# Attention with feature maps: token sums of the key features past 32 standing columns of ones, turned together with the key sums, and projection weights first on the load queue

## The chip, the cores and the metric

One core of a Trainium2 chip runs the whole program. The metric is device time in microseconds (us) from launch to end, as the median of several executions. Engines are named as in the profile: PE (TensorE, matmuls; PEld its weight loads), DVE (VectorE), ACT (ScalarE), POOL (GpSimd) and SP (SyncE, which here only issues DMAs). Each engine takes its instructions in the order in which the program gives them.

## The reference, cut to what matters

```
def phi(x):                                  # x: 8 batches, 8 heads, 576 tokens, 64
    proj = x @ w_phi                         # 64 -> 128 features
    proj = proj - max(abs(proj), last axis)
    return concat([exp(proj), exp(-proj)])   # 256 features
q_p, k_p = phi(q), phi(k)
kv  = einsum('bhsf,bhsd->bhfd', k_p, v)      # key sums, 256 x 64 for each batch and head
z   = sum(k_p, over tokens)                  # token sums, 256 for each batch and head
num = q_p @ kv ; den = q_p @ z + 1e-6
x   = num / den                              # 4608 tokens x 512
x   = (h - tanh(h)) @ w_out, h = x @ w_in    # first expert stage
out = ((x @ w1) * (x @ w2)) @ w3 @ w_out2    # second expert stage
```

Everything is 32-bit floating point. The change concerns `kv`, `z` and the loads at the start; the two expert stages are untouched.

## The kernel before, in words

The attention stage is `attention()`. A *step* is one head of a pair of batches: 1152 tokens in nine tiles of 128. There are 32 steps of keys; the queries of a step run one step behind its keys, so there are 33 passes and 297 tiles. The loop at L412 goes over *slots*, four tiles each, 75 with tiles and a few more to drain. Nine slots make four steps. The order of the work on each engine is the order in which this loop calls the parts; there is no planner.

In slot s, PE gets: `p_pe(s)` (projections of the queries on array rows 0 to 63 and of the keys on rows 64 to 127, L212), `t_pe(s-1)` (transposes of the query projections, L253), `kv_pe(s-2)` (key sums into a PSUM bank `kv`, two column tiles of 64, L290), `o_pe` of a step (numerators, L343, and denominators, L352, one half of the tokens a slot; eight slots of nine have one), and, if a step's key sums were finished in the slot before, `kv_turn` of that step. `kv_turn` transposes the two halves of the key sums with the identity (L325) and multiplies the four key-feature sums `ks`, 128 tokens x 128 features, as weights with one moving column of ones (L329), which gives four columns of token sums.

DVE gets in a slot: `kv_copy` (L320, the finished key sums from PSUM to `kvs`), maximum and difference of the queries (L219, L221), a store copy `st` (L364, every other half; the other halves go to ACT at L366), `kv_out` (L334, the turned sums from PSUM to `kvx`, of the step whose turn was in the slot before), part of the conversion of expert weights, maximum and difference of the keys, the rest of the conversion. `o_pe` of the next step reads `kvx`; in o_pe the denominators read each column of token sums broadcast to 32 weights (L349). ACT takes the exponentials (L232 keys, L274 queries), half of the store copies and parts of the conversion. POOL adds up `ks` over the tiles (L310, L314) and takes parts of the conversion.

`kv` has two PSUM banks, so `kv_pe` of a step needs `kv_out` of the step two before it. `qk` has two buffers; `load_step` (L194) issues the load of the step after next at the end of the slot with a step's last tile, on SP, behind the stores of the slot (two of numerators and four of denominators for each half). `wphi`, the projection weights, is loaded in two halves by ACT's queue (L400), the first `qk` whole by SP.

The last lines of a slot, before:

```
                todo_o = [(st, c, o_pe(st, c)) for st, c in o_at.get(s, [])]
                if turned is not None:
                    kv_turn(turned)
                some(99)
```

Of the kernel before, what the change touches and what calls it, by code (L numbers as in the profile page):

```python
# [8 lines left out]
F32 = mybir.dt.float32  # L9
# [7 lines left out]
B, H, S, D = 8, 8, 576, 64  # L17
F = 128
# [5 lines left out]
PT = 2 * S  # L24
TPP = PT // 128
NPAIR = NBP * H
# [27 lines left out]
def kernel(ctx, tc, qk_in, v_in, w_phi, w_in, w_out, w12, w3t_in, wo2, out):  # L54
    nc = tc.nc
    PE, ACT, DVE, POOL, SP = nc.tensor, nc.scalar, nc.vector, nc.gpsimd, nc.sync
# [14 lines left out]
    ident = const.tile([128, 128], F32, name="ident")  # L71
# [101 lines left out]
    def attention():  # L173
        with ExitStack() as es:
            pool = es.enter_context(tc.tile_pool(name="att", bufs=2))
            one = es.enter_context(tc.tile_pool(name="att1", bufs=1))
# [2 lines left out]
            ps_o = es.enter_context(tc.tile_pool(name="ps_o", bufs=2, space=PSUM))  # L179

            wphi = one.tile([128, F], F32, name="wphi")
            ones = one.tile([128, 1], F32, name="ones")
            n_steps = NPAIR + 1
            n_tiles = n_steps * TPP
            n_slots = (n_tiles + G - 1) // G
# [6 lines left out]
            qk, vv = {}, {}  # L192

            def load_step(st):  # L194
                qk[st] = pool.tile([128, PT], F32, tag="qk", name="qk")
                SP.dma_start(qk[st], qk_in[st])
                if st < NPAIR:
                    vv[st] = pool.tile([128, TPP + 1, D], F32, tag="v", name="v", bufs=3)
                    SP.dma_start(vv[st], v_in[st])
# [3 lines left out]
            def p_pe(g):  # L203
                for what, js in ((pq, q_js(g)), (pk, k_js(g))):
                    if js:
                        what[g] = ps_h.tile([128, 512], F32, tag="h", name="p").rearrange("p (t f) -> p t f", f=F)
                for j, n in enumerate(tiles_of(g)):
                    st, t = where(n)
                    c = slice(t * 128, (t + 1) * 128)
                    for what, js, r in ((pq, q_js(g), 0), (pk, k_js(g), 64)):  # L210
                        if j in js:
                            PE.matmul(what[g][:, j, :], qk[st][r:r + 64, c], wphi[r:r + 64], start=True, stop=True)  # L212
# [13 lines left out]
            def k_exp(g, sgn):  # L226
                js = k_js(g)
                if not js:
                    return
                if sgn == 0:  # L230
                    kp[g] = pool.tile([128, 2, G, F], F32, tag="kp", name="kp", bufs=3)
                ACT.activation(kp[g][:, sgn, span(js)], dk[g][:, span(js)], ACTF.Exp, scale=1.0 - 2 * sgn)  # L232

            def q_parts(g):

                runs = []
                for st, t, j in sorted((where(G * g + j)[0], ORDER[where(G * g + j)[1]], j) for j in q_js(g)):
                    if runs and runs[-1][0] == st and runs[-1][1] + len(runs[-1][2]) == t:
                        runs[-1][2].append(j)
                    else:  # L240
                        runs.append((st, t, [j]))
                return runs

            def t_pe(g):
                runs = q_parts(g)
                if not runs:
                    return
                d = dq.pop(g)
                pt[g] = ps_t.tile([128, 512], F32, tag="tr", name="tr")
                at = 0  # L250
                for st, t, js in runs:
                    for j in js:
                        PE.transpose(pt[g][:, at * 128:(at + 1) * 128], d[:, j, :], ident)  # L253
                        at += 1
# [21 lines left out]
            kv_ps, ks, kvx = {}, {}, {}  # L276
# [39 lines left out]
            kvs = {}  # L316

            def kv_copy(st):
                t = kvs[st] = pool.tile([128, 2 * F], F32, tag="kvs", name="kvs")
                DVE.tensor_copy(t, kv_ps[st][:, :2 * F])  # L320

            def kv_turn(st):
                ps = kv_ps[st]
                for s in range(2):
                    PE.transpose(ps[:, 252 + s * 128:380 + s * 128], kvs[st][:, s * F:(s + 1) * F], ident)  # L325
                for b in range(2):
                    for s in range(2):
                        c = 508 + 2 * b + s
                        PE.matmul(ps[:, c:c + 1], ks[st][:, b, s, :], ones, start=True, stop=True)  # L329
                del kvs[st], ks[st]  # L330

            def kv_out(st):
                t = kvx[st] = pool.tile([128, 260], F32, tag="kvx", name="kvx")
                DVE.tensor_copy(t, kv_ps.pop(st)[:, 252:512])  # L334

            def o_pe(st, c):

                ps = ps_o.tile([128, 512], F32, tag="o", name="o")
                x, w = qp[st], kvx[st - 1]
                for s in range(2):  # L340
                    for b in range(2):
                        c0 = b * S + c * CW
                        PE.matmul(  # L343
                            ps[b * D:(b + 1) * D, :CW], w[:, s * 128 + b * D:s * 128 + (b + 1) * D],
                            x[:, s, c0:c0 + CW], start=s == 0, stop=s == 1,
                        )
                for s in range(2):
                    for b in range(2):
                        z = w[:, 256 + 2 * b + s:257 + 2 * b + s].to_broadcast([128, 32])  # L349
                        for e in range(2):  # L350
                            r, c0 = 64 * b + 32 * e, b * S + c * CW + e * CE
                            PE.matmul(  # L352
                                ps[r:r + 32, CW:CW + CE], z, x[:, s, c0:c0 + CE], start=s == 0, stop=s == 1,
                                tile_position=(0, r),
                            )
                if c:
                    del qp[st], kvx[st - 1]
                return ps
# [37 lines left out]
                for d, fs in zip((0, 2, 3, 3, 4, 4), c):  # L396
                    extra[at + d] += fs

            for i in range(2):
                ACT.dma_start(wphi[i * D:(i + 1) * D], w_phi)  # L400
            load_step(0)
            load_step(1)
            DVE.memset(ones, 1.0)
            o_at = {}
# [3 lines left out]
                    o_at.setdefault(g + 2 + c, []).append((st, c))  # L408
            n_end = n_slots + 8
            ok = lambda g: 0 <= g < n_slots  # L410
            kv_done, turned, todo_o = None, None, []
            for s in range(n_end):  # L412
                x = list(extra[s])

                def some(n):
                    for _ in range(n):
                        if x:
                            x.pop(0)()

                if ok(s):  # L420
                    p_pe(s)
                if kv_done is not None:
                    kv_copy(kv_done)
                if ok(s - 1):
                    k_exp(s - 1, 0)
                    k_exp(s - 1, 1)
                    t_pe(s - 1)
                if ok(s):
                    dq[s] = p_max(s, pq, q_js(s), "q")
                for st, c, ps in todo_o:  # L430
                    bp = o_out(st, c, ps)
                    if bp == NBP - 1:
                        pending.extend([lambda: recip_load(NBP - 1), lambda: recip(NBP - 1)])
                    elif bp is not None:
                        recip_load(bp)
                        extra[s + 4].append(lambda bp=bp: recip(bp))
                if turned is not None:
                    kv_out(turned)
                some(2)
                turned = kv_done  # L440
                if ok(s - 1):
                    q_exp(s - 1, 0)
                    q_exp(s - 1, 1)
                    kv_sum(s - 1)
                kv_done = kv_pe(s - 2) if ok(s - 2) else None
                if ok(s):
                    dk[s] = p_max(s, pk, k_js(s), "k")
                todo_o = [(st, c, o_pe(st, c)) for st, c in o_at.get(s, [])]
                if turned is not None:
                    kv_turn(turned)  # L450
                some(99)
                for n in tiles_of(s) if ok(s) else ():
                    st, t = where(n)
                    if t == TPP - 1 and st + 2 < n_steps:
                        load_step(st + 2)
                i = s - n_slots // 2
                if 0 <= i < 8 * NK:
                    if i % 8 == 0:
                        xa = load_x(0, i // 8)
                    elif i % 8 == 4:  # L460
                        mul_x(*xa)
                    elif i % 8 == 6:
                        split_x(0, i // 8, xa[0])
# [509 lines left out]
    with tc.manual_schedule():  # L973
# [36 lines left out]
        def mul_x(a, r):  # L1010
            POOL.tensor_tensor(a, a, r, ALU.mult)
# [63 lines left out]
```

## Time and profile before

| | us |
|---|---|
| median of three runs | 1761.9 (1760.24 to 1765.2) |
| the profiled execution | 1764.12 |
| its span, first to last instruction | 1762.3 |
| PE busy in the span | 1716.5 (97%) |
| DVE busy | 1331.7 (76%) |
| POOL busy | 1007.1 (57%) |
| ACT busy | 927.2 (53%) |

The profile is of one execution. Attention ends at about 388 us of the span; the expert stages fill the rest. A busy share over the whole span mixes stages, so the rows below are taken from the attention stage, by stretch, by wait and by single instruction. "x16" behind an instruction is the number of rows merged; a 32-bit matmul has two rows, a transpose one.

### The profile page before, as it was taken

How to read it: one execution, taken by the hardware profiler on the slowest of the kernel's cores; microseconds unless marked ns; L12 is line 12 of the kernel's file. 1: busy time of each engine (PE TensorE's matmuls, PEld its weight loads, DVE VectorE, ACT ScalarE, POOL GpSimd, SP SyncE). 2: the span in 40 equal slices, each digit the busy share in tenths (PEclk: the TensorE clock that was granted, in tenths of full speed). 3: DMA queues.
4: the chain of work that ended last, by engine and by line, in shares of the span. 5: the costliest groups of instructions: out<-in, count | busy, mean ns of one | idle time of the engine just before them, and what ended most of it. 6: DMA issues, size and time to landing. Idle time of an engine off the chain costs nothing.

```text
span 1762.3 us, 30387 instructions
## 1 busy us (share of the span) xinstructions
PE 1716.5 (97%) x10608; PEld 1455.0 (83%) x10608; DVE 1331.7 (76%) x1910; ACT 927.2 (53%) x1881; POOL 1007.1 (57%) x966
## 2 busy tenths in 40 slices
PE   7999899999999999999999999999999999999999
PEld 5666666667878788878888878888999999999998
DVE  6777777849888798879899989664766666666664
ACT  4665566646676667666767776544332323222221
POOL 5777677736566677765666667225534353535341
PEclk9999999999999999999999999999999999999999
DMA  4444455522232324233434342635989898989886
GB/s 157 148 149 147 136 171 159 160 61 77 61 114 93 117 78 137 92 129 103 140 105 135 106 137 89 232 117 200 348 261 317 263 315 269 309 269 309 273 268 195
DMA packets 173161, 306.16 MB, mean 174 GB/s; under 512 B 21712, under 2 KB 57936, under 8 KB 173008
## 3 DMA queue, kind: packets, MB, share of 16 engines
q1 hardware_dynamic: 168960, 297.07, 52.1%
q10 hardware_dynamic: 4048, 7.15, 1.1%
q8 instruction: 84, 1.38, 0.3%
q14 instruction: 69, 0.57, 0.1%
HBM read 240.93 MB, written 63.21 MB: 173 GB/s over the span
## 4 chain that ended last, share of the span: by engine, by line
PE 81%; DVE 9%; DMA 4%; issue 2%; POOL 2%; ACT 1%; SPq 1%; DVEq 0%; ACTq 0%; POOLq 0%
PE h L477 18%; PE y L553 18%; PE q L808 14%; PE q L817 7%; PE pa L808 6%; PE p L212 3%; PE o L343 3%; PE o L817 3%; PE h L715 2%; PE kv L290 2%; PE o L352 2%; DVE u L507 1%; DMA qk<-in_qk 1%; DVE t L508 1%; PE tr L253 1%
## 5 line engine op out<-in xcount | busy, mean ns | idle before, releaser
L524 POOL TENSOR_TENSOR gl<-t,gh 128x512 fp32r<-128x512 f32 x144 | 201.5, 1399 | 178.4 <-ACT gh L523 118.5
L553 PE MATMUL y<-gh,w 128*128 128x512 f32 x936 | 237.2, 391 | 3.8 <-ACT gh L523 2.5
L808 PE MATMUL q<-w,w 128*128 128x384 f32 x1152 | 215.1, 334 | 0.0
L553 PEld LDWEIGHTS y<-gh,w 128*128 128x128 f32 x936 | 175.7, 188 | 42.1 <-ACT gh L523 3.5
L507 DVE SCALAR_TENSOR_TENSOR u<-s,u 128x512 f32<-128x512 f32 x144 | 201.0, 1396 | 4.7
L808 PEld LDWEIGHTS q<-w,w 128*128 128x128 f32 x1152 | 201.1, 188 | 0.0
L879 POOL TENSOR_TENSOR xa<-c,c 128x384 f32<-128x384 f32 x48 | 52.1, 1085 | 249.8 <-DVE c L878 179.3
L477 PE MATMUL h<-xa,w 128*128 128x512 f32 x780 | 189.0, 392 | 0.0
L497 ACT ACTIVATE u<-h 128x512 f32<-128x512 f32 x144 | 85.7, 595 | 185.0 <-PE h L477 178.5
L477 PEld LDWEIGHTS h<-xa,w 128*128 128x128 f32 x780 | 147.8, 190 | 31.4 <-issue 0.2
L508 DVE COPY_PREDICATED t<-m,u 128x512 f32<-128x512 uint32 x144 | 166.3, 1155 | 5.0
L219 DVE TENSOR_REDUCE m<-p 128x4 f32<-128x512 f32 (+1 forms) x145 | 98.8, 681 | 79.5 <-PE p L212 79.4
L477 PE MATMUL h<-xb,w 128*128 128x512 f32 x624 | 149.9, 389 | 0.0
L858 ACT ACTIVATE c<-pa 128x384 f32<-128x384 f32 x48 | 23.6, 492 | 237.3 <-PE pa L808 188.0
L232 ACT ACTIVATE kp<-dk 128x512 f32<-128x512 f32 x144 | 83.0, 626 | 109.4 <-DVE dk L221 78.2
L553 PE MATMUL y<-gl,w 128*128 128x512 f32 x468 | 132.0, 394 | 6.5 <-POOL gl L524 6.5
L477 PEld LDWEIGHTS h<-xb,w 128*128 128x128 f32 x624 | 117.1, 188 | 24.5
L135 POOL TENSOR_TENSOR et<-et,eraw 128x256 uint32<-128x256 uint32 x92 | 68.8, 748 | 112.3 <-ACT u L497 35.5
L504 DVE TENSOR_TENSOR t<-h,t 128x512 f32<-128x512 f32 x144 | 98.3, 683 | 42.4 <-ACT t L498 42.2
L505 DVE SCALAR_TENSOR_TENSOR u<-h,u 128x512 f32<-128x512 f32 x144 | 98.6, 684 | 32.8 <-ACT m L500 32.5
L817 PE MATMUL q<-w,w 128*128 128x384 f32 x612 | 112.8, 334 | 0.0
L553 PEld LDWEIGHTS y<-gl,w 128*128 128x128 f32 x468 | 87.2, 188 | 29.2 <-POOL gl L524 11.5
(156 smaller groups left out, 3882.4 us busy)
## 6 DMA issues: line engine op xcount, KB each, us to landing
w<-w_d SPq DMA_DIRECT2D x504, 256.0 KB
w_d<-w SPq DMA_DIRECT2D x84, 256.0 KB
qk<-in_qk SPq DMA_DIRECT2D x33, 576.0 KB
v<-in_v SPq DMA_DIRECT2D x32, 320.0 KB
num_d<-st SPq DMA_DIRECT2D x128, 72.0 KB
xn<-num_d SPq DMA_DIRECT2D x36, 256.0 KB
xb<-y_d SPq DMA_DIRECT2D x24, 384.0 KB
eraw<-in_w SPq DMA_DIRECT2D x32, 256.0 KB
```

Source lines behind the costliest of these rows:

```text
L219: DVE.tensor_reduce(m[:, :n], what[g][:, j], AX.X, ALU.max, apply_absolute_value=True)
L232: ACT.activation(kp[g][:, sgn, span(js)], dk[g][:, span(js)], ACTF.Exp, scale=1.0 - 2 * sgn)
L477: PE.matmul(ps, a[:, kk, :], b[kk], start=m == 0, stop=m == 3 * NK - 1)
L497: ACT.activation(u, h, ACTF.Square)
L504: DVE.tensor_tensor(t, h, t, ALU.subtract)
L505: DVE.scalar_tensor_tensor(u, h, C2, u, ALU.mult, ALU.mult)
L507: DVE.scalar_tensor_tensor(u, s, C0, u, ALU.add, ALU.mult)
L508: DVE.copy_predicated(t, m.bitcast(U32), u)
L524: POOL.tensor_tensor(gl, t, gh.bitcast(F32), ALU.subtract)
L553: PE.matmul(yy[j][d], w[:, d * 128:(d + 1) * 128], x, start=i == 0 and m == 0, stop=i == NFC - 1 and m == 2,)
L808: PE.matmul(ps, w[:, a, c], x[b][:, kk, :], start=start and m == 0, stop=m == 5, skip_group_check=True)
L817: PE.matmul(ps, w[:, a, c], x[:, b, :], start=start and kk == 0 and n == 0, stop=kk == 3 and n == 2, skip_group_check=True,)
```

## The change

The standing column `ones` grows from 1 to 32 columns. `z_pe` is new: for each of the four token sums of a step it makes the 32 columns of ones the weights and moves the 128 features of `ks` past them, each sum on its own column tile of 32, so that 32 equal rows stand in each quarter of the PSUM bank, beside the key sums. It runs at the end of the slot in which the step's key sums were finished. `kv_copy` then takes 384 columns instead of 256, `kv_turn` is three transposes, and `kv_out` takes 384 columns instead of 260. `kv_turn` moves from the end of the slot to behind `t_pe`, and `kv_out` into the same slot, one slot earlier than before. `o_pe` reads 32 real columns instead of a broadcast one. `wphi` is loaded by SP, key half first, ahead of everything; of the first `qk` only the key half is loaded, in two pieces, and of the last only the query half.

```
-            ones = one.tile([128, 1], F32, name="ones")
+            ones = one.tile([128, 32], F32, name="ones")
...
             def load_step(st):
-                qk[st] = pool.tile([128, PT], F32, tag="qk", name="qk")
-                SP.dma_start(qk[st], qk_in[st])
+                t = qk[st] = pool.tile([128, PT], F32, tag="qk", name="qk")
+                if st == 0:
+                    for c in (slice(0, 512), slice(512, PT)):
+                        SP.dma_start(t[64:, c], qk_in[st][64:, c])
+                elif st == NPAIR:
+                    SP.dma_start(t[:64], qk_in[st][:64])
+                else:
+                    SP.dma_start(t, qk_in[st])
...
             def kv_copy(st):
-                t = kvs[st] = pool.tile([128, 2 * F], F32, tag="kvs", name="kvs")
-                DVE.tensor_copy(t, kv_ps[st][:, :2 * F])
+                t = kvs[st] = pool.tile([128, 3 * F], F32, tag="kvs", name="kvs")
+                DVE.tensor_copy(t, kv_ps[st][:, :3 * F])
+
+            def z_pe(st):
+                for j in range(4):
+                    PE.matmul(
+                        kv_ps[st][32 * j:32 * j + 32, 2 * F:3 * F], ones, ks[st][:, j // 2, j % 2, :],
+                        start=True, stop=True, tile_position=(0, 32 * j),
+                    )
+                del ks[st]
 
             def kv_turn(st):
                 ps = kv_ps[st]
-                for s in range(2):
-                    PE.transpose(ps[:, 252 + s * 128:380 + s * 128], kvs[st][:, s * F:(s + 1) * F], ident)
-                for b in range(2):
-                    for s in range(2):
-                        c = 508 + 2 * b + s
-                        PE.matmul(ps[:, c:c + 1], ks[st][:, b, s, :], ones, start=True, stop=True)
-                del kvs[st], ks[st]
+                for s in range(3):
+                    PE.transpose(ps[:, (s + 1) * F:(s + 2) * F], kvs[st][:, s * F:(s + 1) * F], ident)
+                del kvs[st]
 
             def kv_out(st):
-                t = kvx[st] = pool.tile([128, 260], F32, tag="kvx", name="kvx")
-                DVE.tensor_copy(t, kv_ps.pop(st)[:, 252:512])
+                t = kvx[st] = pool.tile([128, 3 * F], F32, tag="kvx", name="kvx")
+                DVE.tensor_copy(t, kv_ps.pop(st)[:, F:4 * F])
...
-                        z = w[:, 256 + 2 * b + s:257 + 2 * b + s].to_broadcast([128, 32])
+                        z = w[:, 2 * F + 32 * (2 * b + s):2 * F + 32 * (2 * b + s + 1)]
...
-            for i in range(2):
-                ACT.dma_start(wphi[i * D:(i + 1) * D], w_phi)
+            for i in (1, 0):
+                SP.dma_start(wphi[i * D:(i + 1) * D], w_phi)
...
                     t_pe(s - 1)
+                if kv_done is not None:
+                    kv_turn(kv_done)
...
-                if turned is not None:
-                    kv_out(turned)
+                if kv_done is not None:
+                    kv_out(kv_done)
                 some(2)
-                turned = kv_done
...
                 todo_o = [(st, c, o_pe(st, c)) for st, c in o_at.get(s, [])]
-                if turned is not None:
-                    kv_turn(turned)
+                if kv_done is not None:
+                    z_pe(kv_done)
```

## Rows read from the trace of the kernel before

**Rows 1.** Busy us (and instructions) by stretch: PE, PEld, DVE, ACT, POOL, clock, DMA, GB/s.
```profile
60.00:350.00 290.00, 272.29 (x3086) 187.40 (x3077) 223.72 (x371) 174.41 (x382) 210.91 (x250) 1.00 0.50 155
...
400.00:1762.00 1362.00, 1350.45 (x6634) 1202.78 (x6634) 1040.77 (x1431) 698.54 (x1386) 739.23 (x644) 1.00 0.56 183
```

**Rows 2.** Waits of PE, 0 to 450 us: total us, times, longest us.
```profile
PE o L343 <- DVE kvx L334: 9.4, 17, 1.3
PE p L212 <- DMA wphi<-in_w_phi: 7.3, 1, 7.3
PE kv L290 <- DVE kvx L334: 6.3, 6, 2.1
PE p L212 <- DMA qk<-in_qk: 2.5, 2, 1.6
```

**Rows 3.** Chain of waits, 39 to 50 us: start us, us, what.
```profile
39.01 0.37 PE kv L325 x2
39.37 0.79 PE kv L329 x8
...
43.22 0.34 DVE kvx L334
...
43.60 1.19 PE o L343 x8
...
46.52 0.58 PE tr L253 x4
...
48.12 0.97 PE o L343 x8
49.09 0.63 PE o L352 x16
```

**Rows 4.** Single lines: count, min/median/max ns, first and last start us, form.
```profile
L320 DVE COPY kvs<-kv x32: 362/415/420, 26.5 to 378.2; 128x256 f32<-128x256 f32 x32
...
L364 DVE COPY st<-o x32: 597/597/607, 42.6 to 388.2; 128x432 f32<-128x432 f32 x32
...
L352 PEld LDWEIGHTS o<-qp,kvx x1024: 105/110/110, 34.0 to 387.7; 128*32 128x32 f32 x171
```

**Rows 5.** Waits of DVE, 30 to 380 us.
```profile
DVE m L219 <- PE p L212: 68.6, 50, 4.0
```

**Rows 6.** Timeline, POOL and PE: start us, us, instruction.
```profile
212.55 1.52 POOL L310 TENSOR_TENSOR ks<-ks,kp 64x256 f32<-64x256 f32 x2
...
220.28 1.16 PE L212 MATMUL p<-wphi,qk 64*128 64x128 f32 x16
```

**Rows 7.** Chain of waits at the start.
```profile
1.53 5.65 DMA wphi<-in_w_phi
```

**Rows 8.** Loads of qk: timeline (SP's issue, PE's wait) and one load in the chain.
```profile
246.00 0.38 SPq L196 DMA_DIRECT2D qk<-in_qk  x1
...
250.67 0.52 PEld L212 LDWEIGHTS p<-wphi,qk 64*128 64x128 f32 x8 [0.29 <-DMA qk<-in_qk]
...
291.86 3.47 DMA qk<-in_qk
```

**Rows 9.** Timeline, kv_copy behind kv_pe's start: first and last of four.
```profile
24.30 1.08 PE L290 MATMUL kv<-kp,v 128*64 128x256 f32 x8
...
26.50 0.41 DVE L320 COPY kvs<-kv 128x256 f32<-128x256 f32 x1
...
303.43 1.08 PE L290 MATMUL kv<-kp,v 128*64 128x256 f32 x8
...
304.06 0.41 DVE L320 COPY kvs<-kv 128x256 f32<-128x256 f32 x1
```

**Rows 10.** Waits, 0 to 450 us, and timeline: ACT's query exponentials, the next transposes.
```profile
ACT qp L274 <- PE o L352: 21.0, 13, 2.1
...
224.77 0.89 ACT L274 ACTIVATE qp<-tr 128x128 f32<-128x128 f32 x4 [1.86 <-PE o L352]
...
226.82 0.66 PE L253 MATMUL tr<-ident,dq 128*128 128x128 f32 x4
```

More of the change, by code (lines that the diff above doesn't have):

```diff
@@ L410, in attention @@
             ok = lambda g: 0 <= g < n_slots
-            kv_done, turned, todo_o = None, None, []
+            kv_done, todo_o = None, []
             for s in range(n_end):
```

## The prediction, made before the changed kernel ran

> **What bounds the kernel now.** I read the busy time by stretch first, then what the matmul engine (PE) waited for, then the chain of waits inside the attention stage, and last the single rows around the edit. Through attention PE is busy 272.29 of 290 us, DVE 223.72, POOL 210.91; behind it, from 400 us on, PE is busy 1350.45 of 1362 [rows 1]. So PE sets the pace on both sides, the later stages contain nothing that the diff touches, and whatever attention ends earlier the whole ends earlier. Of what PE waited for up to 450 us [rows 2], 7.3 us is the start, 9.4 us (17 waits) is o_pe waiting for kvx, 6.3 us (6 waits) is kv_pe waiting for the PSUM bank that kv_out empties, and 2.5 us is a late load of qk. The reader is to see that two of these four name the same DVE copy, L334. The chain [rows 3] shows it in place: DVE reduces p, copies st, copies kvx, and only then the eight matmuls of o_pe begin, with 1.19 us to their end where the unstalled eight take 0.97. The profiled execution took 1764.12 us against its span of 1762.3; the median of the runs shown is 1761.9, 2.2 lower. I make the sum against 1764.1 and carry it over.
>
> **Part 1, the turn itself (PE work, on the path).** A step has one turn; there are 32 [rows 4]. Now it is two transposes, 0.37 us, and four matmuls with the 128x128 key sums as weights and one moving column, eight rows in 0.79 us: 1.16 us [rows 3]. After, kv_turn is three transposes; four cost 0.58 us in t_pe [rows 3], so three cost 0.44. z_pe is four matmuls (eight rows) of 128 columns on four column tiles. The trace has no such row; the nearest is the token-sum part of o_pe, L352: 16 rows of 144 columns on the same four tiles in 0.63 us [rows 3], 0.039 each, so eight cost 0.28 (scaled to 128 columns) to 0.31. If four tiles did not run beside one another, I take the bound from L343, 0.97 us for eight rows of 288 columns, two tiles at a time: 0.97 x 2 x 128/288 = 0.86. I use 0.30, since L352 has the same four tiles and the same width of weights. 1.16 - 0.44 - 0.30 = 0.42 us, 32 times: **-13.4 us**.
>
> Each of L352's 16 rows has a weight load of 0.110 us [rows 4]; together these are 1.76 us, and they pass in 0.63, so loads run beside matmuls of other column tiles. The Trainium skill ("TensorE: Matmul & The Clock Gate", Part 3, The mechanism) says that a weight load overlaps a running matmul only when its row group differs; all tiles here share the row group. By that rule eight loads alone are 0.88 us; the trace disagrees, and I keep 0.30.
>
> **Part 2, kvx one slot (one pass of the loop at L412) earlier (waits, on the path).** kv_copy stays at the head of the next slot; kv_turn moves from that slot's end to behind t_pe, and kv_out into the same slot. o_pe that reads kvx starts at least one slot later, about 5 us, so L334 cannot be last there. The 9.4 and 6.3 us go [rows 2], and the 17 restarts, 1.19 instead of 0.97 [rows 3], give 3.7: **-19.4 us**. What is late next: loads of qk, kvs, and ACT's exponentials (part 5).
>
> **Part 3, DVE and POOL (beside PE).** Both copies grow to 384 columns. From 256 columns at 0.415 us and 432 at 0.597 [rows 4] the slope is 1.03 ns a column: 0.13 us more for each copy, 0.26 us a step, 8.4 us of DVE. It costs nothing where DVE waits for PE, and it does: 68.6 us in 50 slots between 30 and 380 us [rows 5]. Without that cover it would be 8.4 us. z_pe needs POOL's key sums a slot earlier than the old matmuls did. A typical sum starts at 212.55 and ends by 214.1; z_pe would come just ahead of the projection at 220.28 [rows 6], 6 us later, so it waits for nothing. Memset of 32 columns and the contiguous weights in place of a broadcast one in o_pe: same rows, same columns; I take zero. From below, a broadcast load could be what holds L352 above L343's rate (0.97/8 x 144/288/2 = 0.030 against 0.039): up to -9 us; a loss has no row that suggests one.
>
> **Part 4, the start.** Now the first projection waits until wphi, issued at 1.53 on ACT's queue, lands 5.65 us later [rows 7]. After, wphi's two halves are first on SP, then only the key half of the first step, in two pieces; ACT loses two issues before it has work, SP gains three, and the loads of v and of the next qk queued behind them leave about 1.2 us later, with 288 KB less ahead of them. A later qk of 576 KB lands 3.47 us after issue [rows 8]; 64 + 128 KB at some 1.6 us should land by 4.1. So PE starts 3.2 us earlier; if wphi's 5.65 us is its own and not the queue's, it lands at 0.7 + 5.65 = 6.4 and the gain is 0.9; if it lands by 3.5, 3.8. I take **-3.2**, since the loads ahead of it account for the delay. The last step's halved load is waited for by nobody.
>
> On this the Trainium skill ("DMA: Bandwidth & Descriptors", Queues, rings and completion order) speaks against the edit: each DMA engine goes round the queue rows packet by packet, so wphi alone on ACT's row should not have stood behind SP's megabyte. By that rule 5.65 us would be the load's own. No row here shows packets; 5.65 for 64 KB beside 3.47 for 576 KB speaks against the rule as the whole story.
>
> **Part 5, what is given back.** (a) In a period of four steps one projection meets its qk just as it lands. Its issue (246.00) stands on SP behind four stores of st, and PE stood for it until 250.67 [rows 8]. PE will come 1.16 - 0.44 = 0.72 earlier and SP will not; four of seven periods are at that edge: 3 us. (b) kv_turn now waits for kv_copy with kv_pe and o_pe queued behind it on PE, where before it was last. In 4 of 32 slots the copy ended after kv_pe had begun; the first by 26.91 - 24.30 = 2.6, the last by 304.47 - 303.43 = 1.0 us [rows 9]. Five more lead by under 0.5 us and lose that to a faster PE. Part of this pays for waits that come anyway: 5 us. (c) In half of the steps ACT's q exponentials wait for o_pe (13 shown waits) and end at 225.66, 1.16 us before t_pe at 226.82 [rows 10]; that lead is just the turn that leaves. A tie: 1 us, or 5 if each of 16 slips by 0.3. Together **+9**, from 4 to 20.
>
> Sum: -13.4 - 19.4 - 3.2 + 9 = -27.0; 1764.1 - 27 = 1737.1, and on the median's scale **1735**.
>
> **The rivals.** *More is given back*: DVE, ACT and SP's qk loop bind in the slots behind the one without o_pe, and (a) to (c) cost 19 instead of 9. For it, the leads of rows 9 and 10; against it, DVE's 68.6 us of waiting: 1745. *Nothing new is late*: (a) to (c) cost nothing: 1726. *The start gains 0.9*: 1737. *The sums don't overlap* (0.86 for z_pe): +18, 1753; L352 speaks against it. *Other loop*: loads and stores on SP set attention's period whatever PE does, and only the start moves: 1759; against it, PE's rows 2 show only 2.5 us for qk. *The cover goes (slower)*: kv_turn's wait for kv_copy replaces kvx's in every step. Place: behind t_pe, with kv_pe and o_pe held. Price: the mean of rows 9's two, 1.8 us, 32 times, 58 against the 36 gained: +22, 1784. It decides from 36/32 = 1.1 us a step. For it, DVE gets 8.4 us more work in a shorter stage; against it, 28 of 32 copies now end ahead of kv_pe.
>
> **How the numbers follow.** Forecast 0.52, more given back 0.20, start rule 0.10, nothing late 0.08, sums don't overlap 0.03, other loop 0.04, slower 0.03. The range runs from the gross sum with the start at its best and a little of the contiguous load (1722) to the second rival with the start at 0.9 and part of (c) at its bound (1750): 0.90 by these chances. About 0.3%, 5.3 us, is what a measurement can tell from no change: faster 0.93, same 0.04, slower 0.03.
>
> **What would show it.** Right: no wait of o_pe or kv_pe for kvx; eight z rows in about 0.3 us and three transposes in 0.44; first projection near 4.1; qk and kvs as PE's longest waits. Wrong: z rows at 0.1 us each; kvs waits over 1 us in most steps; a first projection after 6; the later stages shorter or longer than now.

## The result and the profile after

The changed kernel took 1738.9 us (median; 1736.4 to 1740.4) beside 1763.4 of the kernel before in the same runs; the ratio is 0.9861, 95% interval 0.9841 to 0.9882. That is 24.5 us less, against a forecast of 27 less (1735, range 1722 to 1750). In a later set of runs the same two gave 1743.1 and 1763.0, ratio 0.9885 (0.9866 to 0.9905). Medians and ratios are of the fast executions; one of six of the variant e4 below took 3424 us and is left out as slow. The profiled execution took 1740.35 us with a span of 1738.6. Line numbers are some ten higher than before.

Busy time by stretch (us and instructions of PE, PEld, DVE, ACT, POOL; clock; DMA; GB/s), to be read against [rows 1]:

```profile
60.00:325.00 265.00, 249.80 (x2988) 168.79 (x2984) 223.25 (x358) 167.13 (x371) 205.53 (x240) 0.98 0.51 163
...
376.00:1738.00 1362.00, 1350.57 (x6636) 1203.11 (x6636) 1043.87 (x1432) 700.38 (x1390) 738.67 (x644) 1.00 0.56 183
```

The second line is the same stretch as the second of [rows 1], 24 us earlier: 1362 us long, PE busy 1350.57 against 1350.45. Nearly the whole gain was made before it. The first matmul of the first expert stage comes at 365.46 us of the span, before at 388.06: 22.6 of the 23.7 us between the two spans. From that matmul to the end the profiled executions of this document take 1372.5 to 1375.0 us, whatever the variant, so the last microsecond is scatter. DVE now works 84% of the attention stretch instead of 77%.

What PE waited for up to 430 us, against [rows 2], and DVE between 30 and 355 us, against [rows 5]:

```profile
PE p L218 <- DMA qk<-in_qk: 18.5, 9, 4.8
PE kv L339 <- DVE kvs L326: 6.1, 7, 2.7
PE tr L259 <- ACT qp L280: 0.6, 2, 0.4
...
DVE m L225 <- PE p L218: 33.3, 44, 4.3
```

No wait for kvx is left. In its place stand waits for qk and kvs, which before were 2.5 and 1.6 us; one of the qk waits, 4.8 us, is now the start. Waits of 2.2 us for dq and 1.4 us for nothing that the profile names, which the kernel before had beside those of [rows 2], are gone too.

The chain of waits inside attention, where PE alone makes it (start us, us, what), against [rows 3]:

```profile
116.84 0.63 PE o L362 x16
117.47 0.22 PE kv L330 x8
117.69 1.09 PE p L218 x16
118.78 0.59 PE tr L259 x4
119.37 0.33 PE kv L339 x3
```

L330 are the new sums, 0.22 us, and L339 the three transposes of the turn, 0.33: 0.55 us a step where it was 1.16. The reader should compare four transposes at 0.59 with three at 0.33, and sixteen rows of 144 columns at 0.63 with eight of 128 at 0.22. Neither is in proportion. The first of each pair comes behind matmuls that lie on other parts of the array (the transposes behind projections on 64 rows, L362 behind tiles of 64 columns); the second follows work of its own tile shape. A fixed 0.15 us at a change of shape accounts for the figures: 0.59 = 0.15 + 4 x 0.11, 0.33 = 3 x 0.11; 0.63 = 0.15 + 16 x 0.030, 0.22 = 8 x 0.027, and before, 0.37 = 0.15 + 2 x 0.11.

Single lines, against [rows 4]:

```profile
L344 DVE COPY kvx<-kv x32: 547/548/557, 27.2 to 359.6; 128x384 f32<-128x384 f32 x32
...
L330 PEld LDWEIGHTS kv<-ks,ones x256: 106/110/110, 20.5 to 357.9; 128*32 128x32 f32 x128
```

The copy of 384 columns takes 0.548 us, as the slope said. Each of the new sums' eight rows has a load of 0.110, 0.88 in all, and they pass in 0.22.

The start, timeline of PE (in brackets the wait before the instruction):

```profile
4.79 4.18 PE L218 MATMUL p<-wphi,qk 64*128 64x128 f32 x18 [4.79 <-DMA qk<-in_qk]
10.66 1.65 PE L218 MATMUL p<-wphi,qk 64*128 64x128 f32 x12 [1.69 <-DMA qk<-in_qk]
...
26.03 0.55 PE L339 MATMUL kv<-ident,kvs 128*128 128x128 f32 x3 [2.72 <-DVE kvs L326]
...
32.12 1.14 PE L353 MATMUL o<-qp,kvx 128*64 128x288 f32 x8
```

The first projection is 2.5 us earlier than before, the first o_pe (32.12 against 32.95) only 0.8: a wait for the second qk and one for kvs, behind DVE's first conversion of weights, take the rest.

The longest wait for qk, timeline (SP's issues, then PE), and below it busy times by stretch with the clock granted, 241 to 243 us:

```profile
231.76 0.36 SPq L159 DMA_DIRECT2D craw<-in_w_in  x1
232.21 0.79 SPq L202 DMA_DIRECT2D qk<-in_qk  x1
...
239.03 1.22 PE L218 MATMUL p<-wphi,qk 64*128 64x128 f32 x8 [4.70 <-DMA qk<-in_qk]
...
241.23 1.98 PE L296 MATMUL kv<-kp,v 128*64 128x256 f32 x8
```

```profile
241.00:243.00 2.00, 2.00 (x12) 1.01 (x12) 1.89 (x3) 1.64 (x3) 2.00 (x3) 0.50 0.54 217
```

The load was issued at 232.21, right behind another of 512 KB, and landed 6.8 us later. Of the loads in [rows 8] one took 3.5 us and the other, at 246.00 and also right behind one of 512 KB, 4.6; the one that corresponds to it in the second profile below took 4.8. Why this one took 2 us longer than those no run shows. PE stood for 4.70 us, and then its clock was at the lower of its two levels, 0.50, that is 1.2 GHz: the same eight matmuls took 1.98 us there and 1.08 once it was back, as in [rows 9]. Up to the end of attention such stretches last 13.6 us in this profile (3.4, 3.4 and 6.8), 3.4 in the one of before. Work at the lower level takes about twice as long (1.98 against 1.08), so the 10.2 us more cost about 5 us, an estimate.

### The profile page after: what moved, and what is told of

Same layout as the page of the kernel before. It is cut to its first block, busy times and chain, and to the rows that moved or that the text cites. A ratio compares the mean times of both kernels' runs of the same rounds, so it can differ in the third digit from the quotient of the medians.

```text
span 1738.6 us, 30470 instructions
## 1 busy us (share of the span) xinstructions
PE 1699.1 (98%) x10640; PEld 1440.4 (83%) x10640; DVE 1342.2 (77%) x1910; ACT 926.3 (53%) x1881; POOL 1009.1 (58%) x966
## 4 chain that ended last, share of the span: by engine, by line
PE 80%; DVE 6%; DMA 5%; SPq 2%; ACT 2%; POOL 2%; issue 2%; DVEq 0%; ACTq 0%; POOLq 0%
PE h L488 18%; PE y L564 18%; PE q L819 14%; PE q L828 7%; PE pa L819 6%; PE o L828 3%; PE p L218 3%; PE kv L296 3%; DMA qk<-in_qk 3%; PE h L726 3%; PE o L353 2%; PE o L362 1%; PE tr L259 1%; DVE u L518 1%; DMA xn<-rden_d 1%
## 5 line engine op out<-in xcount | busy, mean ns | idle before, releaser
L488 PEld LDWEIGHTS h<-xb,w 128*128 128x128 f32 x624 | 117.1, 188 | 24.5
L218 PE MATMUL p<-wphi,qk 64*128 64x128 f32 x1152 | 94.2, 296 | 18.5 <-DMA qk<-in_qk 18.5
```

What stands on the lines that cost most here:

```text
L488: PE.matmul(ps, a[:, kk, :], b[kk], start=m == 0, stop=m == 3 * NK - 1)
```

## The experiments

All carry the kernel before in the same runs; ratios are to it. They were run in three later sets: e1 to e4; the changed kernel again with e5, e6 and e7; e7 again with e8, e9 and e10. The changed kernel stood in the second of these alone, so for the other two the scale is its two ratios, 0.9861 and 0.9885, which differ by 4 us.

**The changed kernel again**

> The changed kernel once more, unchanged, beside its variants on one chip: 1736 to 1740, ratio to the kernel before 0.984 to 0.989; waits for qk 16 to 20 us, for kvs 5 to 8.

1743.1 us, ratio 0.9885 (0.9866 to 0.9905). The time is 3 us above what I expected, the ratio inside it. Waits of PE:

```profile
PE p L218 <- DMA qk<-in_qk: 15.8, 7, 4.8
PE kv L339 <- DVE kvs L326: 5.9, 6, 2.7
```

The wait of 1.7 us for the second qk at the start is not in this profile; its first o_pe still comes at 31.96.

**The start undone (e1)**

```
-            for i in (1, 0):
-                SP.dma_start(wphi[i * D:(i + 1) * D], w_phi)
+            for i in range(2):
+                ACT.dma_start(wphi[i * D:(i + 1) * D], w_phi)
... (load_step as before)
```

> The changed kernel with its start undone: wphi on ACT's queue, first and last qk loaded whole. Forecast of the prediction: the new start is worth 3.2 us, so 1742 against the changed kernel's 1739, first projection near 7.3 instead of 4.8. Rival, read from the two traces: after its early first projection the changed kernel waits 1.7 us for the second qk and 2.7 us for kvs, so nearly all of the gain is gone by the first turn (26.0 against 27.0 before); then 1740, within 1.5 us of the changed kernel.

1740.4 us, ratio 0.9884 (0.9871 to 0.9897): no difference from the changed kernel that can be measured. The first projection comes at 7.11, and the first o_pe at

```profile
32.98 1.14 PE L347 MATMUL o<-qp,kvx 128*64 128x288 f32 x8
```

against 32.12 and 31.96. In the changed kernel the new start is worth at most a microsecond, as the rival said.

**The turn late, new sums and start kept (e2)**

```
+                if turned is not None:
+                    kv_turn(turned)
                 if kv_done is not None:
                     z_pe(kv_done)
... (kv_out one slot later, as before)
```

> The changed kernel with kv_turn back at the end of the next slot and kv_out one slot later, the new token sums and the new start kept. Theory (kvx's place is worth a wait of some 15 us and restarts of 4, less what the earlier PE gives back): waits of o_pe and kv_pe for kvx return with 10 to 16 us, waits for kvs under 1 us, 1749 (1746 to 1753). Rival (the loads of qk set the pace, so the place of the turn hardly matters): 1742 or less, with the waits for qk shrinking by as much as those for kvx grow.

1755.3 us (1748.9 to 1756.3), ratio 0.9960 (0.9947 to 0.9973): only 5 us under the kernel before by the medians, 7 by the ratio. Waits of PE in the profiled execution, the slowest of the six, and the turn in its chain, right behind L362:

```profile
PE o L353 <- DVE kvx L344: 12.4, 17, 1.9
PE p L218 <- DMA qk<-in_qk: 8.3, 6, 4.9
PE kv L296 <- DVE kvx L344: 7.6, 6, 2.2
```

```profile
71.80 0.48 PE kv L339 x3
```

The waits for kvx are 20.0 us where they were 15.7: PE does less in a step and stands longer for DVE instead. It does not do 0.61 us less, as in the changed kernel, but 0.46, since the three transposes take 0.48 us behind tiles of another shape: 1.16 - 0.22 - 0.48. So the place of the turn decides, and the time is 2 us above the upper end that I gave. Of the 15 us that the cheaper turn takes off PE here, 5 to 7 are gained.

**The move alone, on the kernel before (e4)**

```
                     t_pe(s - 1)
+                if kv_done is not None:
+                    kv_turn(kv_done)
... (kv_out in the same slot; old sums, old start)
```

> The kernel before with kv_turn moved behind t_pe and kv_out into the same slot, nothing else: old token sums, old start. Theory (the place of kvx by itself): waits for kvx gone, 19 us gross less some 6 for qk and kvs, 1750 (1746 to 1754). Rival (they are replaced by waits for kvs and qk): 1758 or more.

1751.3 us (1745.9 to 1754.5), ratio 0.9944 (0.9929 to 0.9959): 9 to 10 us under the kernel before. Waits of PE in the profiled execution, the slowest of the five, and the turn in its chain:

```profile
PE p L212 <- DMA qk<-in_qk: 7.9, 6, 2.9
PE kv L325 <- DVE kvs L320: 7.7, 8, 2.6
```

```profile
80.44 0.59 PE tr L253 x4
81.03 0.22 PE kv L325 x2
```

The waits for kvx are gone, and 11.5 us come back under these two names, which had 4.1 before: inside the range of the theory, 1 us above its middle. Two things that I had not named change as well. The old turn's two transposes take 0.22 us behind transposes where they took 0.37 [rows 3]: the move by itself takes a change of tile shape out of every step, 0.15 us, 4.8 in all. And the stretches at the lower clock last 17.1 us instead of 3.4, which costs about 7, estimated as above. By the ratios the two parts alone give 7 and 10 us, 17 together; both at once give 20 to 24. That this is more than the sum is at the edge of the noise in the times. The rows show the exchange: the cheaper work alone is in part eaten by longer waits for kvx (e2), and the move takes those away.

**qk's load ahead of the stores (e3)**

```
                 if ok(s):
                     p_pe(s)
+                    for n in tiles_of(s):
+                        st, t = where(n)
+                        if t == TPP - 1 and st + 2 < n_steps:
+                            load_step(st + 2)
... (the load of v stays at the slot's end)
```

> The changed kernel with the load of the step after next issued on SP right behind the projection that frees its buffer, ahead of the slot's stores, instead of at the slot's end; loads of v stay. Theory (SP's order makes qk late): PE's waits for qk fall from 18.5 us to under 9, start included, the slow stretches of PE's clock behind them go, 1727 (1724 to 1731). Rival (the load is late because it shares the DMA engines with loads of weights and of v): waits stay over 14 us, 1736 or more. Second rival (ACT or DVE is late next): waits for qk go, but waits for kvs or the exponentials take their place, 1734 or more.

1733.6 us, ratio 0.9845 (0.9833 to 0.9858). Waits of PE:

```profile
PE kv L341 <- DVE kvs L328: 12.3, 11, 2.7
PE p L220 <- DMA qk<-in_qk: 6.3, 3, 4.9
```

SP's order was the cause of qk's lateness: beyond the start's 4.9, 1.4 us are left. But of the 9.5 us that qk's waits lost against the changed kernel's second profile 6.4 came back as waits for kvs, the second rival, and the time lies between the two: by the ratios 3 to 7 us less than the changed kernel, where I expected 12. The first expert matmul comes at 355.60 us, 9 us ahead of the second profile's 364.60, and past the start no stretch at the lower clock is left in attention.

**kv_copy ahead of the conversion (e6)**

```
                     z_pe(kv_done)
+                    kv_copy(kv_done)
                 some(99)
... (not at the head of the next slot)
```

> The changed kernel with kv_copy put ahead of the slot's last conversion steps on DVE, right behind the keys' difference. Theory (kvs is late where DVE still converts weights): waits for kvs fall from 6.1 us to under 3, 1736 (1733 to 1739), since waits for qk stay. Rival (DVE now stands for z_pe with the conversion behind it, and the queries' maximum slips): 1740 or more, with new waits of the projection for DVE.

1741.8 us, ratio 0.9876 (0.9859 to 0.9893): no difference, as the rival said. Waits of PE:

```profile
PE p L218 <- DMA qk<-in_qk: 17.5, 9, 4.8
...
PE p L218 <- DVE dq L227: 2.4, 2, 1.9
PE kv L339 <- DVE kvs L326: 2.0, 3, 1.2
```

The waits for kvs fall from 5.9 to 2.0 as the theory had it, and the time doesn't move: qk takes 1.7 us more, the projections' waits for DVE 2. Here, taking away the smaller wait alone only lengthened the larger.

**Both (e7, and once more as c_e7)**

The edits of e3 and e6 together, and nothing else.

> Both at once: qk's load behind the projection (as in e3, where waits for kvs rose to 12.3 us while those for qk fell to 6.3) and kv_copy ahead of the conversion. Theory (each wait is set by its own queue): waits for qk under 7, for kvs under 6, 1727 (1724 to 1731). Rival (DVE as a whole is at its limit once PE is not held up, so its waits only move): 1732 or more, the kvs waits replaced by waits of projections or transposes for DVE or ACT.

1723.7 us, ratio 0.9773 (0.9756 to 0.9790). Again, in the last set:

> The changed kernel with qk's load behind the projection and kv_copy ahead of the conversion once more (as e7), beside what follows on one chip: 1722 to 1727, ratio to the kernel before 0.975 to 0.980.

1721.8 us, ratio 0.9783 (0.9767 to 0.9799), 0.8 to 1.1% under the changed kernel by the ratios, the fastest here. Waits of PE in e7, and busy times of its attention stretch:

```profile
PE p L220 <- DMA qk<-in_qk: 5.5, 2, 4.8
PE kv L341 <- DVE kvs L328: 3.8, 5, 1.2
```

```profile
30.00:356.00 326.00, 319.65 (x3832) 217.64 (x3821) 275.44 (x443) 209.65 (x461) 255.17 (x297) 1.00 0.52 156
```

PE is busy 98% of it, the clock granted is 1.00 throughout, and past the start only 0.7 us of waits for qk are left. So nearly all that the changed kernel gave back was due to two queue orders, not to a limit of DVE, which does the same work here.

**kv_turn behind kv_pe (e5)**

```
-                kv_done = kv_pe(s - 2) if ok(s - 2) else None
+                turned, kv_done = kv_done, kv_pe(s - 2) if ok(s - 2) else None
+                if turned is not None:
+                    kv_turn(turned)
+                    kv_out(turned)
```

> The changed kernel with kv_turn behind kv_pe instead of behind t_pe (kv_out behind it, ahead of the keys' maximum). Theory (a change of PE's tile shape costs about 0.15 us, read from rows of the changed kernel: four transposes 0.59 where the shape changes before them, three more 0.33 where it doesn't): the turn stands between work of another shape on both sides, each step gains two changes of shape, 0.3 us, 32 times 10 us of PE work, the three transposes of the turn take 0.45 to 0.5 instead of 0.33 and the o_pe matmuls behind them some 0.15 more; waits for kvs fall from 6 to about 3; 1743 (1740 to 1747). Rival (the shape costs nothing, what counts is the lead of kv_copy, 1 us longer here): 1735 or less, the turn at 0.33.

1741.0 us, ratio 0.9874 (0.9856 to 0.9892): no difference in the time. The chain of waits:

```profile
182.87 1.01 PE kv L296 x8
183.88 0.48 PE kv L339 x3
184.36 1.12 PE o L353 x8
```

The same three transposes take 0.48 instead of 0.33, and the o_pe matmuls behind them 1.12 instead of 0.97: 0.15 for each change of tile shape, as read from the changed kernel's rows. Where the time goes is seen at the turn's first weight load, in the timelines of the changed kernel and of e5:

```profile
119.10 0.36 PEld L339 LDWEIGHTS kv<-ident,kvs 128*128 128x128 f32 x3
```

```profile
183.81 0.31 PEld L339 LDWEIGHTS kv<-ident,kvs 128*128 128x128 f32 x3 [0.39 <-DVE dq L227]
```

In the changed kernel the load starts 0.11 us ahead of its first matmul (119.21), beside the transposes before it; in e5 it starts together with it (183.81), so nothing of it is hidden. Over the steps the median lead is 0.11 us there and none here. Whether the engine empties first or only the load comes late these rows don't separate.

The 10 us that this makes are there as work of PE. Up to the first expert matmul PE is busy 346.54 us in e5 and 341.82 in the changed kernel's second profile, although its stretches at the lower clock last 10.2 us instead of 17.1: about 8 us more at equal clock. Against it stand 3.2 us less of waiting (for kvs 1.7 instead of 5.9, and that at the start) and some 3 us from the clock, so the first expert matmul comes 1.5 us later and the time shows no difference.

**kv_copy late: the slower rival made on purpose (e8)**

```
                 if ok(s):
                     dq[s] = p_max(s, pq, q_js(s), "q")
+                if kv_done is not None:
+                    kv_copy(kv_done)
+                    kv_turn(kv_done)
... (not at the head of the slot, not right behind t_pe)
```

> The changed kernel with kv_copy held behind the queries' maximum and difference on DVE, so that kv_turn, kv_pe and o_pe stand for it in every step: the prediction's slower rival made on purpose. Its price: the copy ends about 3.0 us after the slot's projection begins (1.09 + 1.42 + 0.5) and PE wants it after 1.7, so 1.3 us a step, 32 times 42, less what it takes over of the waits for qk and kvs (10 to 15): 27 to 32 more than the changed kernel, 1768 (1762 to 1775), slower than the kernel before. Rival (PE's wait is hidden because DVE and qk's loads set the pace): under 1750.

1780.1 us, ratio 1.0105 (1.0091 to 1.0120): slower than the kernel before. Waits of PE, and one step of the chain of waits:

```profile
PE kv L339 <- DVE kvs L326: 51.9, 32, 4.0
```

```profile
107.53 0.70 DVE m L225
...
108.25 0.69 DVE dq L227
108.95 0.47 DVE kvs L326
...
109.47 0.55 PE kv L339 x3
```

Every one of the 32 steps waits, 1.6 us on average. The prediction's slower case had 1.8 us and 1784. My price before the run, 1.3 us a step, was too low by a fifth, and the time came out above my range. The waits for qk were taken over almost whole: 0.8 us are left beyond the start.

**The start undone, with the later waits gone (e9)**

The edit of e1, made on e7.

> e7 with the start undone: wphi on ACT's queue, first and last qk whole. Theory (the new start is worth what it moves the first projection by, 2.3 us from 7.1 to 4.8, where no later wait takes it back, and in e7 the first o_pe comes at 28.7 instead of 32): first o_pe near 31, 2 to 3 us more than e7, 1726.5. Rival (loads and weight conversions set the first 30 us in any case): first o_pe within 0.7 us of e7's, no difference in the time.

1724.8 us against 1721.8 of c_e7; ratio 0.9792 (0.9778 to 0.9806) against 0.9783, intervals that overlap. First o_pe in the timeline of e9, and of c_e7:

```profile
32.48 1.17 PE L349 MATMUL o<-qp,kvx 128*64 128x288 f32 x8
```

```profile
28.54 1.14 PE L355 MATMUL o<-qp,kvx 128*64 128x288 f32 x8
```

3.9 us by the rows, more than the 2.4 by which the first projection moved (7.15 to 4.73). Some 1.7 of it is the clock: in e9 it is at its lower level for 3.4 us just ahead of this row (0.57 on average from 29 to 33 us), in c_e7 it is 1.00 from 25 to 29. At the first expert matmul 3.4 us are left (349.97 against 346.55). The time agrees with the theory but doesn't settle it alone.

**qk's load ahead of the stores, in the kernel before (e10)**

The edit of e3, made on the kernel before.

> The kernel before with nothing but qk's load issued behind the projection, ahead of the stores. Theory (qk became late because PE got faster, it was at the edge before): waits for qk 2.5 us fall to near 0, 2 to 4 us less, 1759 (1757 to 1762), so that most of what e3 and e7 gain belongs to the change's give-back. Rival (qk's place in the queue always cost, hidden in waits given to others): 1752 or less.

1759.4 us, ratio 0.9990 (0.9982 to 0.9999). Waits of PE:

```profile
PE o L345 <- DVE kvx L336: 9.4, 17, 1.3
```

No wait for qk is left, those of o_pe for kvx stay, and the gain is 2 us. qk's place cost next to nothing while PE was held by kvx; it became the longest wait when the change set PE free.

## Why the prediction was right, point by point

**What bounds the kernel**: right. PE is as busy in the later stages as before, 1350.6 of 1362 us, and the gain is in attention.

**Part 1, -13.4**: the right term, too small; it measured 1.16 - 0.22 - 0.33 = 0.61 us a step, **-19.5**. Both new pieces were scaled from groups that carry the 0.15 us of a change of tile shape, the turn from four transposes (0.44 instead of 0.33), the sums from L362's like before (0.30 instead of 0.22), although both now stand behind work of their own shape. Of the 0.61 only 0.46 is the cheaper work (e2). The other 0.15, 4.8 us in 32 steps, comes with the move, which puts the turn behind transposes (e4); no part of the prediction had it. The Trainium skill ("TensorEngine Tiling (Array Packing)", Key Properties) says that changing the tiling mode drains TensorE; it gives no price, and the rows here do: 0.15 us, shown again in e5. Had the four transposes been read beside the two of the old turn (0.58 and 0.37), the fixed part would have come out of [rows 3] alone. The Trainium skill's rule on weight loads, which the prediction cites, was rightly set aside for these column tiles, since 0.88 us of loads pass in 0.22. The contiguous weights changed nothing: sixteen rows of o_pe still take 0.63.

**Part 2, -19.4**: right. No wait for kvx is left; e2 brings them back.

**Part 3, nothing**: right on average. DVE's copies cost what the slope said, and its waits for PE fell from 68.6 to 33.3 us; z_pe waits for nothing.

**Part 4, -3.2**: right on what held wphi up, wrong in what the shift was worth. PE did start at 4.8, near the 4.1 named, and not at the 6.4 of the case in which wphi's 5.65 us is its own. The DMA packets show why: the kernel before up to 3.4 us and from there to 7.2 (its queues of SP, q1, and of ACT, q10), and the changed kernel up to 3.4 us:

```profile
q1 hardware_dynamic: 92, 0.42, 46.6%
```

```profile
q10 hardware_dynamic: 160, 0.07, 7.0%
```

```profile
DMA packets 163, 0.07 MB, mean 21 GB/s; under 512 B 32, under 2 KB 160, under 8 KB 163
```

In the changed kernel the 160 packets of wphi's 64 KB had moved by 3.4 us, with nothing ahead of them. In the kernel before, where its two halves were issued at 0.91 and 1.53 us, none had moved by then; SP's queue had moved 0.42 MB, and wphi's packets went between SP's until about 7 us. The prediction read the Trainium skill ("DMA: Bandwidth & Descriptors", Queues, rings and completion order) as if going round the queues packet by packet meant no delay for a small load on a queue of its own. The trace does not speak against that rule, since packets of both queues moved between 3.4 and 7.2 us (435 of SP's); it shows that a small load waits all the same when large loads are ahead on the other queue.

The step that failed comes after this: at the first o_pe only 0.8 us were left. I carried the shift through without asking what is last at the first turn: DVE's copy behind its first weight conversion, 2.7 us late. In c_e7, where the copy goes first, the start is worth 3.9 us at that point and 3.4 at the end of attention.

**Part 5, +9**: (a) 3 us for qk was mis-sized. Beyond the start, qk's waits take 12.0 us by the rows (18.5 less 4.8 and 1.7) against 2.5: 9.5, and about 5 more for PE's clock, which goes to its lower level behind the longest of them. I counted one load a period at its edge by 0.72 us, with a fixed time to land. The lead of PE grew by the larger saving of the turn and by the kvx waits too, and the time to land was not fixed (4.6 to 6.8 us where the load follows one of 512 KB). That it is SP's order is shown by e3. (b) 5 us for kvs: about right, 6.1 less 2.7 at the start, plus 0.22 us for each of six restarts, 4.7. (c) 1 us: right, 0.6.

Sum by what was measured: -19.5 - 19.4 - 0.8 + 9.5 + 5 + 4.7 + 0.6 = -19.9, against 22.6 at the first expert matmul. The 2.7 us left over are found when PE's time up to that matmul is split into work and waiting (before, then after; the figure behind the comma is PE's busy time):

```profile
0.00:388.06 388.06, 356.79 (x3937) 245.24 (x3937) 285.44 (x472) 222.62 (x484) 266.93 (x322) 1.00 0.46 144
```

```profile
0.00:365.46 365.46, 340.06 (x3968) 230.58 (x3969) 294.36 (x472) 221.21 (x484) 270.44 (x322) 0.98 0.48 151
```

Work falls by 16.7 us: -19.5 for the turn, -3.7 of old restarts, +1.3 of new ones and about +5 for the clock make -16.9. Waiting falls by 5.9 us, from 31.3 to 25.4, and the rows of waits add up to 30.9 and 25.2 of it. Among them are the 3.6 us for dq and for nothing named that are gone, which neither the prediction nor the sum above has. Against them, the waits at the start add up to 1.1 us less gain than the 0.8 read at the first o_pe. Together these are 2.5 of the 2.7.

That the forecast came out better than its terms is luck: Part 1 missed by 6 us one way and qk by 12 the other, the start paid 2.4 us less, and some waits left that nobody had counted.

**The rivals**: of the cases, "more is given back", 1745, came nearest in its mechanism: it put (a) to (c) at 19 us, and they measured 19.8. In number, with 27 us less, the forecast missed the 24.5 of the first set by 2.5 and the 19.8 of the second by 7. *The start gains 0.9*, with 24.7, was nearest in the first set, though not by its own mechanism, since wphi did land early; *More is given back*, with 17, was nearest in the second. The slower rival's mechanism is shown by e8: it pays 1.6 us in each step, above the break-even of 1.1, and ends 18.7 us slower than before, where (1.6 - 1.1) x 32 would be 16.

## What to carry to other kernels

Shorten the work and the wait behind it together: alone they gave 7 and 10 us here, both 20 to 24, and the next two queues in line another 14 to 20. When a faster engine is forecast, list every load and copy that lands just in time and ask which queue it stands in; a load that costs nothing now (2 us, e10) can cost 14 by the rows afterwards. Scale a matmul group's time to another length only after taking off what it pays for a change of tile shape in front of it.

## What the hardware showed that was not expected

A change of tile shape between matmul groups costs about 0.15 us (three transposes 0.33 behind their own shape, 0.48 behind another; two 0.22 and 0.37), and with it the first weight load no longer runs ahead. A wait can cost more than its length: around the end of a stand of 4.7 us PE's clock was at 1.2 GHz for 6.8 us, and eight matmuls took 1.98 instead of 1.08. A 576 KB load took from 3.5 to 6.8 us to land, the three read here that were issued right behind one of 512 KB 4.6, 4.8 and 6.8. 64 KB on a queue of its own had landed only 5.65 us after the issue of its second half, with large loads ahead on the other queue; first on that queue, it had moved by 3.4 us of the span.
